# Hash attention and a gated feed-forward on one core: the softmax divisors of a pair summed in one group of four matmuls

## The chip, the cores and the metric

The kernel runs on one core of a Trainium2 chip. The metric is the device time of one execution in microseconds (us). Ten runs of the kernel before have a median of 919.51 us, from 918.42 to 920.82. One further number is used below: the execution that the profiler recorded took 918.83 us, and its span, from the first to the last instruction, is 917.0 us.

## The reference, cut to what matters

```python
# attention: 4 batches x 8 heads, S = 768, head_dim = 64, 6 hash bits
q_bits, k_bits = (q @ proj > 0), (k @ proj > 0)
mask = bucket(q_bits)[:, :, :, None] == bucket(k_bits)[:, :, None, :]
scores = np.where(mask, q @ k.T / sqrt(64), -1e9)
attn = exp(scores - max)
attn = attn / (attn.sum(-1) + 1e-9)
x = (attn @ v)                      # -> (3072, 512)
# feed-forward
h = x @ w_in                        # (3072, 2048)
g = h * erf(softplus(h))
out = g @ w_out                     # (3072, 512)
```

What the change touches is `attn.sum(-1)`: for each query the sum of its 768 exponentials, by which the row of `attn @ v` is divided.

## The kernel before, in words

The 32 heads are worked off as 16 **pairs**; the two heads of a pair (called `ab`) share the 128 partitions, 64 each. The 768 queries of a pair come in two **halves** of 384 (`HS`); `h = 0..31` counts halves over all pairs, so pair `i` has the even half `2i` and the odd half `2i+1`. The 768 keys come in six blocks of 128, and one **score stage** `n` (four of them per pair) does three of these blocks for one half.

The stages, and who does them:

- `bits_of` (L812, PE, tensor `bits`): the hash bits of a whole pair, four matmuls of 32 output rows and 384 columns, on four column quarters of the array. From there: `sign_of` (ACT, L821) writes `sg`, `weigh_bits` (DVE, L831) scales half of it, `leave_bits` (POOL, L841) sends it to DRAM (`bd`), and `place_bits` (POOL, L850) brings it back in two DMAs into one of two mask tiles `both`, which the score stages of that pair read.
- `score` (L550, PE, tensor `st`): for each key block a matmul on the mask (`both`, bf16) and one on `q` and `k` (f32), for both heads side by side. Transposed scores: keys on partitions, queries in columns.
- `exponential` (L568, ACT): `st` to `e_all`, a ring of nine blocks.
- `weigh` (L631, PE, tensor `av`): the exponentials times `v`, twelve f32 matmuls for each of the two heads in one half.
- `sum_keys` (L619, DVE): adds the six blocks of exponentials of a half to one tile of 128 partitions (`x_sum` for even halves, a part of `x` for odd ones). What is left is a sum over the partitions.
- `divisor` (L666, PE, tensor `z_ps`): that sum, by matmuls with a matrix of ones. It stands once for each half. Four matmuls, one on each column quarter: two heads times two parts of 192 queries. `keep_divisor` (L679, ACT) copies `z_ps` to `z`.
- `spread`, `gather`, `invert`, `ungather`, `widen` (SP and DVE, tensors `zd`, `zc`, `rd`, `r`), once per pair: the divisors go through DRAM to be laid over 128 partitions, are inverted, and come back broadcast. `normalise` (DVE, L752) applies them, `send` (SP, `xs`) stores the result.
- Beside this, 32 **pieces** of the feed-forward's weights are fetched by POOL (`raw`, L456) and converted by ACT (L470, L477) and DVE (L484 to L532), two pieces per pair. A piece is fetched only after the piece two before it is converted.

**What sets the order.** PE's order in the attention is written out by hand in the list `order`, and every PE operation comes after the one before it. The other engines' orders come from `arrange`, a planner that goes through the operations with a cost and a rank each and appends what can start first; on each engine instructions then run in that order. POOL's queue holds `leave_bits`, `place_bits` and the weight fetches. In the order before, half `h` reads

```python
score(2h+1), score(2h+2)      # "st"
bits((h+3)//2)                # odd h only
divisor(h-1)                  # z of the half before
weigh(2h), weigh(2h+1)        # "av"
```

so in time `st, bits, z, av` (odd half) and `st, z, av` (even half) alternate. The last half's divisor stands in the feed-forward (`late`). The feed-forward, with matmuls `M` and `X` (L1183, L1323), begins at 324.5 us of the span and is not touched.

Of the kernel before, what the change touches and what calls it, by code (L numbers as in the profile page):

```python
# [54 lines left out]
F32 = mybir.dt.float32  # L55
# [8 lines left out]
P = 128  # L64
# [129 lines left out]
def kernel(  # L194
# [11 lines left out]
    nc = tc.nc  # L206
    B, H, S, D = v.shape
    NBIT = proj2.shape[1] // 2
    NPAIR = B * H // 2
# [3 lines left out]
    HS = S // 2  # L213
# [23 lines left out]
    ones = const.tile([P, D], F32, name="ones")  # L237
# [15 lines left out]
    for ab in range(2):  # L253
        rows = slice(ab * D, ab * D + D)
        nc.vector.tensor_copy(
            out=proj_sb[rows, ab * QR : ab * QR + NBIT],
            in_=proj_in[rows, ab * NBIT : (ab + 1) * NBIT],
        )
    row = const.tile([P, 1], F32, name="row")
    nc.gpsimd.dma_start(out=row, in_=bucket)  # L260
    steps = const.tile([P, 8], F32, name="steps")
    for c, (end, factor) in enumerate(
# [12 lines left out]
            out=steps[:, c : c + 1],  # L275
# [23 lines left out]
    def bank(name):  # L299
        return misc.tile([P, 512], F32, name=name, tag="bank")  # L300
# [115 lines left out]
    def attention():  # L416
        NS = NPAIR * 4
        with (
# [19 lines left out]
            pairs = {}  # L438
            raws = {}
            NH = NPAIR * 2  # L440
# [150 lines left out]

            def last_sum(h):
                return len(sum_steps(h)) - 1 if h >= 0 else 0
# [45 lines left out]
            def home(i, what):  # L639

                if i < NPAIR - 1:
                    shape, bufs = {"x": (S, 3), "z": (HS, 1), "r": (S, 2)}[what]
                    return xst.tile([P, shape], F32, name=what, tag=what, bufs=bufs)
                rows = blocks[1][:, :, :].rearrange("p k t -> p (k t)")
                c = {"x": S, "z": 2 * S, "r": 0}[what]
                return rows[:, c : c + (HS if what == "z" else S)]
# [8 lines left out]
                    accum_out=stats[:, n, i, half : half + 1],  # L655
                )

            def divisor(h):


                i, half = divmod(h, 2)
                d = pairs[i]
                z = d["z_ps"] = bank("z_ps")[:, 0 : HS // 2]
                for n in range(4):
                    ab, part = divmod(n, 2)
                    nc.tensor.matmul(  # L666
                        out=z[n * QR : (n + 1) * QR, :],
                        lhsT=ones[:, 0:QR],
                        rhs=d["sum", half][:, 0, ab, part * HS // 2 : (part + 1) * HS // 2],
                        start=True,  # L670
                        stop=True,
                    )

            def keep_divisor(h):
                i, half = divmod(h, 2)
                d = pairs[i]
                if half == 0:
                    d["z"] = home(i, "z")
                nc.scalar.copy(  # L679
                    out=d["z"][:, half * HS // 2 : (half + 1) * HS // 2], in_=d.pop("z_ps")  # L680
                )

            def leave(h):

# [19 lines left out]
            def spread(i):  # L704

                d = pairs[i]
                zd = d["zd"] = dram.tile([2, 4, HS // 2], F32, name="zd", tag="zd")
                d["zc"] = small.tile([P, 2 * S // P], F32, name="zc", tag="zc")
                nc.sync.dma_start(
                    out=zd.rearrange("h n c -> n h c"),  # L710
                    in_=d["z"][0 : 3 * QR + 1 : QR, 0:HS].rearrange("n (h c) -> n h c", h=2),
                )

            def gather(i):
                d = pairs[i]
                nc.sync.dma_start(
                    out=d["zc"],
                    in_=d.pop("zd")
                    .rearrange("h n c -> (h n c)")
                    .rearrange("(p c) -> p c", c=2 * S // P),  # L720
                )

# [56 lines left out]
            for n in range(WARM):  # L779
                nc.tensor.matmul(  # L780
                    out=bank("warm")[:, 0 : 2 * P],
                    lhsT=warm[:, 0:P],
                    rhs=warm[:, P:HS],
                    start=True,
                    stop=True,
# [5 lines left out]
            NH = NPAIR * 2  # L791
            ops = []

            def op(fn, args, engine, cost, rank, after=(), **more):
                name = (fn.__name__,) + args
                ops.append(Op(name, engine, cost, rank, lambda: fn(*args), after=after, **more))

            def pe(fn, args, cost, after=()):
                if chain:
                    after += (chain[-1],)  # L800
                op(fn, args, "PE", cost, (0, len(chain)), after, late=0.25)
                chain.append((fn.__name__,) + args)
# [58 lines left out]
            chain = []  # L861
            order = [("score", 0)]
            for h in range(NH):
                order += [("score", n) for n in (2 * h + 1, 2 * h + 2) if n < NS]
                if h == 0:
                    order.insert(3, ("bits", 1))
                if h % 2 and (h + 3) // 2 < NPAIR:
                    order.append(("bits", (h + 3) // 2))
                if h >= 1:
                    order.append(("divisor", h - 1))  # L870
                order += [("weigh", 2 * h), ("weigh", 2 * h + 1)]
            slots = []
            for what, n in order:
                if what == "score":
                    i = n // 4
                    after = (("place_bits", i),)
                    if n == 0:
                        for c in range(2):
                            pe(plain, (n, c), 0.66)
                    for c in range(GC):  # L880
                        free = (slots[-3],) if len(slots) >= 3 else ()
                        pe(score, (n, c), 0.82 if n or c == 2 else 0.17, after + free)
                        slots.append(("exponential", n, c))
                elif what == "bits":
                    pe(bits_of, (n,), 0.92, (("start_pair", n), slots[-3]))
                    slots.append(("sign_of", n))
                elif what == "divisor":
                    pe(divisor, (n,), 0.42, (("sum_keys", n, last_sum(n)), ("keep_divisor", n - 1)))
                else:
                    h = n // 2  # L890
                    after = (("exponential", n, GC - 1),)
                    if n % 2 == 0:
                        after += (("leave", h - 1), ("leave_plain", (h - 1) // 2))
                    pe(weigh, (n,), 2.02, after)
# [18 lines left out]
            for h in range(NH):  # L913
                for k, (blocks_, _, _, where) in enumerate(sum_steps(h)):
                    after = tuple(("exponential", 2 * h + b // GC, b % GC) for b in blocks_)
                    after += (("sum_keys", h, k - 1), ("sum_keys", h - 1, last_sum(h - 1)))
                    if k == 0:
                        after += (("divisor", h - 2),)
                        if h == NH - 2:
                            after += (("measure", NPAIR - 3, 0, 1),)  # L920
                    op(sum_keys, (h, k), "DVE", 1.72 if where == 2 else 0.92, (1, 2 * h + 1, k), after)
            for h in range(NH - 1):
                i = h // 2
                op(
                    keep_divisor,
                    (h,),
                    "ACT",
                    0.34,
                    (0, 2 * h, -1),
                    (("divisor", h), ("spread", i - 1)),  # L930
                )
            for h in range(NH):
                i = h // 2
# [3 lines left out]
            for i in range(NPAIR):  # L937
                n = 4 * i
# [765 lines left out]
    with tc.manual_schedule():  # L1704
        late = attention()
        feed_forward(judge, late)
# [57 lines left out]
```

## Time and profile before

| | us |
|---|---|
| median of 10 runs | 919.51 |
| profiled execution | 918.83 |
| its span | 917.0 |
| PE busy in the span | 904.3 |
| DVE busy | 819.7 |
| ACT busy | 768.4 |
| `z_ps` matmuls (L666), passes x duration | 256 x 0.33 to 0.34, four at a time |
| `bits` matmuls (L812), passes x duration | 120 x 0.50, four at a time |
| copies `z<-z_ps` (L679) | 30 x 0.33 |

PE is TensorE's matmuls, PEld its weight loads, DVE VectorE, ACT ScalarE, POOL GpSimd, SP SyncE; a q behind a name means the engine's sequencer or queue. A row of the timeline gives the start and the length in us, the engine, the line, the operation, the tensors written and read, the shape, how many are merged, and in brackets the idle time before it and what ended it. An f32 matmul shows as two passes. Matmuls of one row can lie side by side on parts of the array, so lengths are not added up: the distance from one start to the next is what a stage costs.

### The profile page before, as it was taken

To read this page: it belongs to the slowest core of one execution; us is meant where nothing else is said; L and a number is where in the kernel's file an instruction comes from. 1 tells how busy PE (TensorE), PEld (TensorE's weight loads), DVE (VectorE), ACT (ScalarE), POOL (GpSimd) and SP (SyncE) were. 2 spreads that over 40 slices of the span, in tenths; PEclk is the share of its full clock that TensorE was granted. 3 is DMA by queue.
4 is the path that set the end of the run, shared out by engine and by line. 5 is a ranking of instruction groups with operands and counts; after the bars stand their busy time and mean duration, and the time that the engine had idled before them with its cause. 6 is when DMAs were issued, how large, how long until landed. Compare 5 with 4: busy or idle time off the path is not lost.

```text
span 917.0 us, 13120 instructions
## 1 busy us (share of the span) xinstructions
PE 904.3 (99%) x5006; PEld 658.7 (72%) x5006; DVE 819.7 (89%) x1020; ACT 768.4 (84%) x1002; POOL 46.7 (5%) x83
## 2 busy tenths in 40 slices
PE   9999999999999999999999999999999999999997
PEld 4444444444444478888888888888888888888885
DVE  4899999999898979899999799989899889988995
ACT  5788887788887839999998998899989997899892
POOL 1211111111111000000000000000000000000000
PEclk9999999999999999999999999999999999999999
DMA  8455567655673131102022112211121121011201
GB/s 205 118 154 161 158 181 196 184 144 161 178 199 107 59 122 64 46 1 104 12 70 80 36 46 69 81 35 46 70 81 35 35 75 40 36 35 46 69 35 49
DMA packets 62966, 83.05 MB, mean 91 GB/s; under 512 B 34174, under 2 KB 47342, under 8 KB 62896
## 3 DMA queue, kind: packets, MB, share of 16 engines
q1 hardware_dynamic: 56672, 64.08, 24.0%
q0 software_dynamic: 6064, 17.86, 6.1%
q8 instruction: 41, 0.67, 0.3%
q14 instruction: 29, 0.24, 0.1%
q10 hardware_dynamic: 160, 0.20, 0.1%
HBM read 64.71 MB, written 17.40 MB: 90 GB/s over the span
## 4 chain that ended last, share of the span: by engine, by line
PE 95%; DVE 2%; ACT 1%; DMA 1%; issue 0%; POOL 0%; DVEq 0%; ACTq 0%; POOLq 0%
PE M L1323 31%; PE X L1183 28%; PE st L550 16%; PE av L631 13%; PE M L1183 3%; PE z_ps L666 1%; PE bits L812 1%; ACT e_all L568 1%; PE warm L780 1%; DMA raw<-in_w_in_dram 0%; DVE e L1237 0%; DMA bd<-sg 0%; DVE h L1265 0%; DMA both<-bd 0%; PE bits L373 0%
## 5 line engine op out<-in xcount | busy, mean ns | idle before, releaser
L1250 DVE SCALAR_TENSOR_TENSOR e<-w,e 128x1024 f32<-128x1024 f32 x144 | 173.4, 1220 | 5.8 <-ACT w L1246 3.0
L568 ACT ACTIVATE e_all<-st 128x768 f32<-128x768 f32 x192 | 151.2, 813 | 14.6 <-PE st L550 14.6
L1246 ACT ACTIVATE w<-w,cq 128x1024 f32<-128x1024 f32 x144 | 160.8, 1145 | 1.9
L550 PE MATMUL st<-q,k 64*128 64x384 f32 x768 | 155.2, 483 | 0.0
L1323 PE MATMUL M<-w_out_sb,h 128*128 128x256 f32 x576 | 140.2, 379 | 0.4 <-DVE h L1265 0.4
L631 PE MATMUL av<-e_all,v 128*64 128x385 f32 (+1 forms) x768 | 131.1, 490 | 0.0
L1183 PE MATMUL X<-x,w_in_sb 128*128 128x256 f32 x512 | 121.1, 379 | 0.0
L1323 PEld LDWEIGHTS M<-w_out_sb,h 128*128 128x128 f32 x576 | 109.2, 190 | 15.9 <-DVE h L1265 1.1
L1183 PEld LDWEIGHTS X<-x,w_in_sb 128*128 128x128 f32 x512 | 97.0, 190 | 13.8 <-ACT h L1201 0.6
L631 PEld LDWEIGHTS av<-e_all,v 128*64 128x64 f32 x768 | 52.3, 136 | 67.5 <-issue 66.9
L1323 PE MATMUL M<-wt,S 128*128 128x256 f32 x384 | 93.4, 379 | 0.4 <-DVE S L1280 0.4
L550 PEld LDWEIGHTS st<-q,k 64*128 64x128 f32 x768 | 68.3, 188 | 34.6 <-issue 34.0
L1183 PE MATMUL X<-x_sum,w_sum 128*128 128x256 f32 x344 | 81.7, 380 | 1.8 <-ACT h L1201 1.8
L1323 PEld LDWEIGHTS M<-wt,S 128*128 128x128 f32 x384 | 72.9, 190 | 10.7 <-DVE S L1280 0.8
L1183 PEld LDWEIGHTS X<-x_sum,w_sum 128*128 128x128 f32 x344 | 65.0, 190 | 12.0 <-ACT h L1201 3.3
L1201 ACT COPY h<-X 128x512 f32<-128x512 f32 x85 | 49.1, 577 | 22.1 <-PE X L1183 21.2
L1227 DVE SCALAR_TENSOR_TENSOR w<-w,e 128x1024 f32<-128x1024 f32 x48 | 58.4, 1221 | 9.7 <-ACT w L1222 9.6
L550 PE MATMUL st<-both 64*128 64x384 bf16 x384 | 63.2, 324 | 1.7 <-DMA both<-bd 1.5
L1265 DVE TENSOR_TENSOR h<-h,e 128x1024 f32<-128x1024 f32 x48 | 58.0, 1220 | 5.8 <-ACT e L1261 5.5
L1241 ACT ACTIVATE w<-e 128x1024 f32<-128x1024 f32 x48 | 50.5, 1051 | 13.2 <-DVE e L1237 12.9
L1237 DVE TENSOR_TENSOR e<-e,w 128x1024 f32<-128x1024 f32 x48 | 57.5, 1219 | 2.7 <-ACT e L1233 2.6
L1205 DVE TENSOR_TENSOR h<-X,h 128x512 f32<-128x512 f32 x65 | 44.8, 690 | 16.3 <-PE X L1183 15.3
(133 smaller groups left out, 1376.6 us busy)
## 6 DMA issues: line engine op xcount, KB each, us to landing
wt<-wt SPq DMA_DIRECT2D x24, 768.0 KB, 4.1
raw<-in_w_out_dram POOLq DMA_DIRECT2D x16, 512.0 KB, 4.1
raw<-in_w_in_dram POOLq DMA_DIRECT2D x14, 512.0 KB, 4.5
v<-in_v_dram SPq DMA_DIRECT2D x32, 192.0 KB, 4.7
xs<-x SPq DMA_DIRECT2D x16, 384.0 KB, 2.6
q<-in_qkT_dram SPq DMA_DIRECT2D x30, 192.0 KB, 4.1
k<-in_qkT_dram SPq DMA_DIRECT2D x30, 192.0 KB, 4.2
r<-rd SPq DMA_DIRECT2D x30, 192.0 KB, 3.5
```

The lines of the kernel that those rows point to most:

```text
L550: nc.tensor.matmul(out=st[:, ab, 0:HS], lhsT=d["k" + src][rows, keys], rhs=d["q" + src][rows, cols], start=(part == 0), stop=(part == 1),)
L568: nc.scalar.activation(out=e[:, :, 0:HS], in_=st[:, :, 0:HS], func=AF.Exp, scale=scale)
L631: nc.tensor.matmul(out=d["av"][rows, 0:w], lhsT=d["v"][:, g * GC + c, rows], rhs=e[:, ab, 0:w], start=(g == 0 and c == 0), stop=(g == 1 an ...
L1183: nc.tensor.matmul(out=d[where][:, u, :], lhsT=a[:, kc, f : f + P], rhs=b[:, kc, :], start=(first and u == 0 and kc == 0), stop=(last and ...
L1201: nc.scalar.copy(out=quarter(p, q), in_=st[p][where])
L1227: nc.vector.scalar_tensor_tensor(out=w, in0=w, scalar=-1.0, in1=st[p]["e", v], op0=ALU.add, op1=ALU.subtract)
L1237: nc.vector.tensor_tensor(out=s, in0=s, in1=st[p].pop(("w", v)), op=ALU.subtract)
L1241: nc.scalar.activation(out=z, in_=st[p]["s", v], func=AF.Square)
L1246: nc.scalar.activation(out=q, in_=z, func=AF.Square, bias=cq[:, j : j + 1])
L1250: nc.vector.scalar_tensor_tensor(out=s, in0=st[p].pop(("q", v, j)), scalar=ERF_Q[j][1], in1=s, op0=ALU.add, op1=ALU.mult,)
L1265: nc.vector.tensor_tensor(out=h, in0=h, in1=st[p].pop(("s", v)), op=ALU.mult)
L1323: nc.tensor.matmul(out=banks[name][:, sub, :], lhsT=a[:, u, sub * P : (sub + 1) * P], rhs=b[:, u, :], start=(c == 0 and k == 0), stop=(c = ...
```

## The change

The divisor of a whole pair is made at once. Four matmuls again, on four column quarters, but now a quarter is one half and one head with all its 384 queries. It stands in the odd half's wake: at the beginning of the next even half, ahead of its scores, and the bits of the pair after the next stand right before it, so that the order is

```python
# even h, from 2 on
bits((h+2)//2); divisor(h-1)                  # both halves of pair (h-1)//2
score(2h+1), score(2h+2); weigh(2h), weigh(2h+1)
# odd h
score(2h+1), score(2h+2); weigh(2h), weigh(2h+1)
```

The last pair keeps a divisor per half, each on two quarters of 384 queries. `keep_divisor` copies 384 columns once instead of 192 twice, the DRAM tile `zd` becomes four rows of 384, and the planner gets the new costs and dependences: the sums of an even half begin only after the divisor of the pair before.

```diff
-            def divisor(h):
-                i, half = divmod(h, 2)
-                d = pairs[i]
-                z = d["z_ps"] = bank("z_ps")[:, 0 : HS // 2]
-                for n in range(4):
-                    ab, part = divmod(n, 2)
-                    nc.tensor.matmul(
-                        out=z[n * QR : (n + 1) * QR, :],
-                        lhsT=ones[:, 0:QR],
-                        rhs=d["sum", half][:, 0, ab, part * HS // 2 : (part + 1) * HS // 2],
+            def divisor(h, halves=None):
+                d = pairs[h // 2]
+                halves = halves or ((h % 2,) if h >= NH - 2 else (0, 1))
+                z = d["z_ps"] = bank("z_ps")[:, 0:HS]
+                for half in halves:
+                    for ab in range(2):
+                        row = (2 * half + ab) * QR
+                        nc.tensor.matmul(
+                            out=z[row : row + QR, :],
+                            lhsT=ones[:, 0:QR],
+                            rhs=d["sum", half][:, 0, ab, :],
...
-                nc.scalar.copy(
-                    out=d["z"][:, half * HS // 2 : (half + 1) * HS // 2], in_=d.pop("z_ps")
-                )
+                rows = slice(half * D, half * D + D) if h >= NH - 2 else slice(0, P)
+                nc.scalar.copy(out=d["z"][rows, :], in_=d.pop("z_ps")[rows, :])
...
             for h in range(NH):
+                if h and h % 2 == 0:
+                    if (h + 2) // 2 < NPAIR:
+                        order.append(("bits", (h + 2) // 2))
+                    order.append(("divisor", h - 1))
                 order += [("score", n) for n in (2 * h + 1, 2 * h + 2) if n < NS]
                 if h == 0:
                     order.insert(3, ("bits", 1))
-                if h % 2 and (h + 3) // 2 < NPAIR:
-                    order.append(("bits", (h + 3) // 2))
-                if h >= 1:
+                if h == NH - 1:
                     order.append(("divisor", h - 1))
                 order += [("weigh", 2 * h), ("weigh", 2 * h + 1)]
...
-                    pe(divisor, (n,), 0.42, (("sum_keys", n, last_sum(n)), ("keep_divisor", n - 1)))
+                    pe(
+                        divisor,
+                        (n,),
+                        0.7,
+                        (("sum_keys", n, last_sum(n)), ("keep_divisor", n - (2 if n % 2 else 1))),
+                    )
...
                     if k == 0:
-                        after += (("divisor", h - 2),)
+                        after += (("divisor", h - (1 if h % 2 == 0 else 2)),)
...
-            for h in range(NH - 1):
+            for h in (*range(1, NH - 2, 2), NH - 2):
                 i = h // 2
                 op(
                     keep_divisor,
                     (h,),
                     "ACT",
-                    0.34,
-                    (0, 2 * h, -1),
+                    0.48,
+                    (0, 2 * h + 1, -1),
```

More of the change, by code (lines that the diff above doesn't have):

```diff
@@ L656, in measure @@
                 )
-            def divisor(h):
-                i, half = divmod(h, 2)
-                d = pairs[i]
-                z = d["z_ps"] = bank("z_ps")[:, 0 : HS // 2]
-                for n in range(4):
-                    ab, part = divmod(n, 2)
-                    nc.tensor.matmul(
-                        out=z[n * QR : (n + 1) * QR, :],
-                        lhsT=ones[:, 0:QR],
-                        rhs=d["sum", half][:, 0, ab, part * HS // 2 : (part + 1) * HS // 2],
-                        start=True,
-                        stop=True,
-                    )
+            def divisor(h, halves=None):
[9 more added lines that the diff above has]
+                            rhs=d["sum", half][:, 0, ab, :],
+                            start=True,
+                            stop=True,
+                        )
             def keep_divisor(h):
@@ L676, in keep_divisor @@
                 d = pairs[i]
-                if half == 0:
+                if "z" not in d:
                     d["z"] = home(i, "z")
-                nc.scalar.copy(
-                    out=d["z"][:, half * HS // 2 : (half + 1) * HS // 2], in_=d.pop("z_ps")
-                )
+                rows = slice(half * D, half * D + D) if h >= NH - 2 else slice(0, P)
+                nc.scalar.copy(out=d["z"][rows, :], in_=d.pop("z_ps")[rows, :])
             def leave(h):
@@ L706, in spread @@
                 d = pairs[i]
-                zd = d["zd"] = dram.tile([2, 4, HS // 2], F32, name="zd", tag="zd")
+                zd = d["zd"] = dram.tile([4, HS], F32, name="zd", tag="zd")
                 d["zc"] = small.tile([P, 2 * S // P], F32, name="zc", tag="zc")
[L709 to L712, printed above, removed]
+                nc.sync.dma_start(out=zd, in_=d["z"][0 : 3 * QR + 1 : QR, :])
             def gather(i):
@@ L718, in gather @@
                     in_=d.pop("zd")
-                    .rearrange("h n c -> (h n c)")
+                    .rearrange("h c -> (h c)")
                     .rearrange("(p c) -> p c", c=2 * S // P),
@@ L887, in attention @@
                 elif what == "divisor":
-                    pe(divisor, (n,), 0.42, (("sum_keys", n, last_sum(n)), ("keep_divisor", n - 1)))
+                    pe(
[3 more added lines that the diff above has]
+                        (("sum_keys", n, last_sum(n)), ("keep_divisor", n - (2 if n % 2 else 1))),
+                    )
                 else:
```

## The prediction

> **What bounds the kernel.** I read the page's busy times and chain first, then the list of PE's waits, then PE's timeline over one pair, and last the timelines of DVE and POOL beside it.
>
> ```profile
> PE 904.3 (99%) x5006; PEld 658.7 (72%) x5006; DVE 819.7 (89%) x1020; ACT 768.4 (84%) x1002; POOL 46.7 (5%) x83
> PE 95%; DVE 2%; ACT 1%; DMA 1%; issue 0%; POOL 0%; DVEq 0%; ACTq 0%; POOLq 0%
> ```
>
> PE is the bound: what shortens its row of stages shortens the kernel, as long as nothing that it waits for comes later. PE's own waits are 1.5 us on `both<-bd` (pair 1), 0.6 us before the feed-forward, and little more. From 66 us to the end of the attention it does not wait once, and repeats this (cost of a stage = distance to the next start):
>
> ```profile
> 106.83 0.81 PE L550 MATMUL st<-q,k 64*128 64x384 f32 x4
> 107.57 0.52 PE L812 MATMUL bits<-q,proj_q 128*32 128x384 f32 x2
> ...
> 107.92 0.49 PE L812 MATMUL bits<-q,proj_q 128*32 128x384 f32 x2
> ...
> 108.24 0.51 PE L666 MATMUL z_ps<-x_sum,ones 128*32 128x192 f32 x8
> 108.68 4.09 PE L631 MATMUL av<-e_all,v 128*64 128x384 f32 x24
> 112.71 0.34 PE L550 MATMUL st<-both 64*128 64x384 bf16 x2
> ...
> 116.75 0.33 PE L550 MATMUL st<-both 64*128 64x384 bf16 x2
> 116.92 0.81 PE L550 MATMUL st<-q,k 64*128 64x384 f32 x4
> 117.66 0.53 PE L666 MATMUL z_ps<-x,ones 128*32 128x192 f32 x8
> 118.12 4.10 PE L631 MATMUL av<-e_all,v 128*64 128x385 f32 x24
> 122.15 0.34 PE L550 MATMUL st<-both 64*128 64x384 bf16 x2
> ```
>
> bits 0.67, z 0.44, av 4.03, st 4.95, z 0.46, av 4.03, and the st before it 4.95: 19.53 us a pair. Each stage ends in a switch of the array's shape (the forms 64\*128, 128\*32, 128\*64), and that is not free. A score block takes 0.81, but the last, 116.75 to 117.66, takes 0.91: 0.10 for st to z. The two rounds of `bits` are 0.35 and 0.32 long, so a 384-column round is 0.32 and the first after a switch 0.02 to 0.03 more. z has two rounds of half that, 0.32, and costs 0.44: 0.12 for z to av. av has twelve rounds of 0.32 (3.86) and costs 4.03: 0.17 for its slow first round and the switch to st.
>
> **The change, part by part.** (1) *Four quarters of 384 instead of twice four of 192.* The columns streamed are the same: twice 0.32 before, once 0.65 after. (2) *The order.* Before there are six switches in a pair (st-bits, z-av, av-st, st-z, z-av, av-st), after it five (av-bits, z-st, st-av, av-st, st-av); bits to z is no switch either way. With each stage's cost as now: bits 0.67, z 0.32 + 0.32 + 0.12 = 0.76, then st 4.95, av 4.03, st 4.95, av 4.03: 19.39 us. That is 0.14 less a pair, for the 15 pairs with a joint divisor **-2.10 us**. av-bits, z-st and st-av stand nowhere in the trace of before; by the neighbouring switches one switch is worth 0.09 (bare) to 0.17 (with the slow first round of av), so the term lies between -1.4 and -2.6. I take the sum of the rows. (3) *The last pair* fills only two quarters with 384 columns: 0.65 instead of 0.32, twice, once before the last av and once inside the feed-forward, both on PE's path: **+0.64 us**.
>
> [...] The rows: the rounds of 192 columns are half as long as those of 384 (z 0.32 for two, `bits` 0.32 for one), so fewer and longer matmuls gain nothing in themselves. [...]
>
> (4) *POOL's queue.* The built order has two weight fetches ahead of the third pair's bits, where before the second of them stood behind `place_bits`. That one cost something:
>
> ```profile
> 58.80 1.14 POOL L456 DMA_DIRECT2D raw<-in_w_in_dram  x2
> 63.35 0.43 DVE L484 TENSOR_SCALAR top<-raw 128x512 int32<-128x512 int32 x1 [0.74 <-DMA raw<-in_w_in_dram]
> 63.41 0.69 ACT L470 ACTIVATE keep<-raw 128x512 f32<-128x512 f32 x1 [3.51 <-DMA raw<-in_w_in_dram]
> ```
>
> ACT stood still 3.51 us behind it, its exponentials came late, and PE's score stage at 63.25 took 5.26 instead of 4.95. Fetched at about 54 us, the piece is there in time: **-0.31 us** on PE (bounds 0 and -0.31), and DVE gets 0.74 us ahead, 1.1 with the 0.39 us that it waits for ACT just after.
>
> (5) *New wait one: z needs the odd half's sums earlier.* The divisor stood 5.0 us behind the odd av; now it follows that av at 0.67 (the bits). In front of everything: the next scores, exponentials and copies queue behind this matmul. DVE is packed (19.2 to 19.4 us busy in every 20 us from 80 to 160 us), so its sums end where its fixed order lets them end. In the built order the work ahead of each odd sum is the same as before to within 0.1 us, except for three pairs where it is 0.4 to 1.4 us less. So sums keep their times, while PE comes earlier by 1.11 us (the bits and z that left the first odd half) and 0.14 for each pair. The tightest pair:
>
> ```profile
> 89.15 4.09 PE L631 MATMUL av<-e_all,v 128*64 128x384 f32 x24
> 92.16 0.32 DVE L831 TENSOR_SCALAR sg<-sg,weight_q 64x384 bf16<-64x384 bf16 x1
> 92.51 0.96 DVE L619 TENSOR_TENSOR x<-x 128x768 f32<-128x768 f32 x1
> ```
>
> The sum ends at 93.47, or 93.1 without the `sg` row, which the built order puts behind it. PE's av would end at 93.18 - 1.84 (1.11 + 0.31 + 0.14 x 3) = 91.3 and z want the sum at 92.0: 1.1 us of waiting, less DVE's 0.7 to 1.1 of lead. The next tightest (190.6) adds 0.3 or nothing, since a wait of PE moves all that comes later. Bounds 0 and 1.4.
>
> (6) *New wait two: the bits leave PE 4 us later* against the scores that need them. DVE's `weigh_bits` runs 3.5 to 4.5 us later in the built order; then
>
> ```profile
> 113.59 0.32 DVE L831 TENSOR_SCALAR sg<-sg,weight_q 64x384 bf16<-64x384 bf16 x1
> 114.20 0.55 POOL L841 DMA_DIRECT2D bd<-sg  x1 [7.30 <-DVE sg L831]
> 118.62 1.15 POOL L850 DMA_DIRECT2D both<-bd  x2 [3.87 <-PE z_ps L666]
> both<-bd POOLq DMA_DIRECT2D x30, 21.0 KB, 3.6
> ```
>
> 0.3 + 4.4 + 0.6 + 3.6 = 8.9 us from the end of `weigh_bits` to the landed mask. The first score on it begins 0.67 + 0.76 + 4.95 + 4.03 + 2.5 = 12.9 us after its bits began. `weigh_bits` would end (its row's place between two sums, with DVE's times of before) 3.9 to 5.5 us after the bits began, so 7.5 to 9.2 us are left, 7.5 to 7.9 in five pairs. With DVE's lead that becomes 8.6 to 9.0. It is a close thing: 0 to 1.4 us by the median trip; with the shortest DMAs (1.9 and 2.1 of 3.6) nothing. The loads of `q`, `k`, `v`, which begin where the odd av ends, lie beside the first DMA as now but have mostly landed by the second, so I lean to the short side. (5) and (6) do not add up: who waits for one has more room for the other. I take **+0.3 us** for both together; the bounds are 0 and 3.5 (1.4 and 2.1, the longest trip of 9.6 in 7.5 us, without any lead).
>
> [...]
>
> (7) *At nothing:* ACT's one copy of 384 for two of 192 (0.33 each), 80% busy there; the round of `zd`, `zc`, `rd`, `r`, whose spread now starts some 4 us earlier while its DVE rows stand about 3 us earlier; later `place_bits` push every second weight fetch back by 3 to 4 us, and its piece still lay 3.4 to 8 us unused. If that cover goes, ACT and DVE wait a few tenths.
>
> Sum: -2.10 + 0.64 - 0.31 + 0.3 = **-1.47 us**. Against the profiled execution 918.83 - 1.47 = 917.4; that run lies 0.7 below the median of 919.51, so the median to expect is **918.0 us**. Measurement can tell about 0.2% here, 1.84 us; the forecast is within it.
>
> **Rivals.** *A, the full gain:* no new wait, a switch worth up to 0.17: -1.8 to -2.3 us, 917.5 at the median. For it: DVE's lead; against: the two tight places. *B, slower, by the mask's trip:* at the second half of the odd score stage PE waits for `both<-bd`. Every us that the trip exceeds its room costs PE one us, once. If DVE gets no lead and the trip is as long as the longest now, the waits are 3.5 us and the sum is -1.46 + 3.5 = +2.0: 921.5. It decides from 1.8 us of waits on (no gain), from 3.6 on it is slower by 0.2%. Against it: such a trip must coincide with the tightest pairs. *C, not four at a time:* the last two quarters wait for DVE and the first two do not, and they could run one after the other, 0.65 more a pair, +9.7 - 1.5: 927.7. Against it: the `bits` have a wait before their third matmul too and take 0.67.
>
> **Chances.** Forecast, -0.5 to -1.84: 0.47; A 0.34; waits that eat the gain without turning it, 0.08; B 0.08; C 0.03. So faster by over 0.2% 0.34, within 0.55, slower 0.11. Range 916.8 to 920.6: A's gain with a low median at one end, most of the waits' bounds at the other.
>
> **What would show it.** In the profile after: 128 passes on L666 of about 0.49; distances bits-z 0.67, z-st 0.76, st-av 4.95, and 19.39 a pair; no `raw` wait near 63 us. Wrong would be: PE waits for `x<-x` at z (5), for `both<-bd` in the odd scores (6), or a st-av distance over 5.05.

## The result, and the profile after

The changed kernel takes 924.33 us (median of 14 runs, 922.23 to 927.04), the kernel before 919.55 us beside it on the same chips (50 runs). The ratio is 1.0051, with a 95% interval of 1.0041 to 1.0061: slower by half a per cent, outside the predicted range. The profiled execution took 925.31 us with a span of 923.5, 6.5 us more than the one of before. In the texts on record below, T1, T2 and so on are the theories of the time; each is told in words here.

The page of the changed kernel, its busy row and the shares of its chain of waits (followed back from the last instruction to whatever released each step); those of before stand in the prediction:

```profile
PE 905.7 (98%) x4878; PEld 658.0 (71%) x4878; DVE 819.7 (89%) x1020; ACT 768.8 (83%) x987; POOL 47.3 (5%) x83
PE 90%; DVE 5%; DMA 3%; SPq 1%; ACT 1%; issue 0%; POOL 0%; DVEq 0%; ACTq 0%; POOLq 0%
```

PE's busy time has hardly moved (904.3 before), but its share of the chain has fallen from 95% to 90%, and DMA has 3% where it had 1%: PE now waits for something. The part that the change meant is as it was worked out. PE's timeline over one pair of the changed kernel:

```profile
108.19 4.09 PE L631 MATMUL av<-e_all,v 128*64 128x384 f32 x24
112.21 0.52 PE L808 MATMUL bits<-q,proj_q 128*32 128x384 f32 x2
...
112.88 0.49 PE L666 MATMUL z_ps<-x_sum,ones 128*32 128x384 f32 x2
112.90 0.49 PE L666 MATMUL z_ps<-x,ones 128*32 128x384 f32 x2
...
113.64 0.34 PE L550 MATMUL st<-both 64*128 64x384 bf16 x2
...
118.59 4.10 PE L631 MATMUL av<-e_all,v 128*64 128x385 f32 x24
```

av to bits is 4.02, bits to z 0.67, z to st 0.76, st to av 4.95. An undisturbed pair takes 19.39 us instead of 19.53. The two z of one round (112.88 and 112.90) start beside each other on different column quarters. What is new stands in the list of PE's waits:

```profile
PE st L550 <- DMA both<-bd: 4.0, 1, 4.0
```

One wait of 4.0 us for a mask: it is pair 9's, in the second half of an odd score stage, the place that rival B named. PE's timeline there (in brackets the idle time ahead of the row and what ended it):

```profile
182.94 0.81 PE L550 MATMUL st<-q,k 64*128 64x384 f32 x4
187.77 0.67 PE L550 MATMUL st<-both 64*128 64x384 bf16 x2 [4.01 <-DMA both<-bd]
188.06 1.65 PE L550 MATMUL st<-q,k 64*128 64x384 f32 x4
```

The rows after the wait are twice as long as their like (0.67 for 0.33, 1.65 for 0.81). Sums by 4 us stretches tell why; the columns are the stretch, its length, busy time of PE, PEld, DVE, ACT and POOL, the granted clock (the share of its full speed at which TensorE was clocked), the busy share of the DMA engines and GB/s:

```profile
184.00:188.00 4.00, 0.23 (x2) 0.17 (x4) 3.83 (x10) 0.61 (x1) 0.04 (x1) 0.89 0.99 359
188.00:192.00 4.00, 4.00 (x20) 2.52 (x21) 3.86 (x4) 2.25 (x5) 0.56 (x1) 0.68 0.66 184
```

The clock is 0.89 and 0.68 in two stretches of 4 us, 1.72 us of clock missing, which is 3.4 us at half clock; in stretches of 1 us from 187 on it is 0.57, 0.50, 0.50 and 0.72, and 1.00 in the ones on either side. The stage of 181.16 takes 10.58 us instead of 4.95: 4.01 of standing still and 1.62 of slow clock. The DMA share of 0.99 points at the cause of the wait. SP's queue and POOL's queue in the changed kernel at that time:

```profile
181.91 0.43 SPq L330 DMA_DIRECT2D x<-xs  x1
```

```profile
182.32 1.15 POOL L846 DMA_DIRECT2D both<-bd  x2 [4.17 <-PE st L550]
```

and in the kernel before:

```profile
176.03 1.57 SPq L330 DMA_DIRECT2D x<-xs  x1
```

```profile
176.18 1.15 POOL L850 DMA_DIRECT2D both<-bd  x2 [4.53 <-DMA bd<-sg]
```

`x<-xs` is `load_x`, 1 MB of the feed-forward's first input. In the changed kernel it goes out 0.4 us ahead of the mask's way back, and the chain of waits has 5.4 us for that 21 KB transfer, where the median of its kind in this run is 2.1:

```profile
182.32 5.40 DMA both<-bd
```

Before, the two go out together too (176.03 and 176.18), but there the two transfers of the mask landed in 2.6 and 3.0 us, and they were sent some 6.5 us ahead of their use. So a mask issued behind the load is not always late: before, the load's row lasts 1.57 us and the mask's begins 0.15 us into it; in the changed kernel the load's lasts 0.43 us and is all but over when the mask's begins. No run shows why the one mask took 3 us and the other 5.4.

A table of the time from the end of the score stage that starts at 22 us (so that the first loads don't count) to the feed-forward's first product. Stretches are distances from one stage's start to the next:

| | from | to | us | PE's stages that are longer than regular, extra us |
|---|---|---|---|---|
| before | 29.14 | 324.46 | 295.32 | st 63 +0.31 |
| changed | 29.61 | 329.81 | 300.20 | z 92 +1.03; st 123 +0.27; z 171 +0.10; st 181 +5.63; z(30) +0.31 |

Before, less 15 x 0.14, less the 0.31 at 63 us, plus the last column's 7.34 gives 300.25: nothing is left over (z(30) is the z of half 30, the last pair's first). Behind this the last pair's second half adds 0.31, and the rest of the 6.5 us lies in the start (0.47) and behind the last products (0.8).

### The profile page after: what moved, and what is told of

The parts are those of the page before. It is cut to its first block, busy times and chain, and to the rows that moved or that the text cites. A ratio compares the mean times of both kernels' runs of the same rounds, so it can differ in the third digit from the quotient of the medians.

```text
span 923.5 us, 12846 instructions
## 1 busy us (share of the span) xinstructions
PE 905.7 (98%) x4878; PEld 658.0 (71%) x4878; DVE 819.7 (89%) x1020; ACT 768.8 (83%) x987; POOL 47.3 (5%) x83
## 4 chain that ended last, share of the span: by engine, by line
PE 90%; DVE 5%; DMA 3%; SPq 1%; ACT 1%; issue 0%; POOL 0%; DVEq 0%; ACTq 0%; POOLq 0%
PE M L1326 31%; PE X L1186 27%; PE st L550 14%; PE av L631 12%; PE M L1186 3%; PE z_ps L666 1%; PE bits L808 1%; DVE x L619 1%; DMA both<-bd 1%; SPq L358 1%; DMA q<-in_qkT_dram 1%; DMA zd<-z 1%; DVE x_sum L619 0%; DMA bd<-sg 0%; DVE e L1240 0%
```

## The experiments

The medians here stand beside runs of the kernel before on the same chip; a ratio is to those.

**1. The changed kernel, with x's load late.** The load moves behind the widening of pair 13, about 305 us; nothing else.

```diff
-            op(load_x, (0,), "SP", 1.1, (1, 0), (("send", JP - 1), ("start_pair", 10)), late=4.0)
+            op(load_x, (0,), "SP", 1.1, (1, 0), (("send", JP - 1), ("widen", NPAIR - 3)), late=4.0)
```

> The changed kernel with one difference: the load of the feed-forward's first input block (1 MB, x<-xs) stands behind the widening of pair 13, near 305 us, instead of just ahead of the way back of pair 9's mask. Theory T1 (one collision: mask 9 queues behind that load, PE stands 4.0 us, and its clock is halved for 3.4 us after): the stall of 5.6 us in the score stage at 181 us is gone, all st-av distances 4.95 but small ones, median 918.6 to 919.6. Rival T2 (the moved bits are simply too late, some other mask will be late instead): another wait on both<-bd of over 1 us appears and the time stays above 922.

920.70 us, ratio 1.0015 (1.0002 to 1.0029). The waits of PE in this run:

```profile
PE st L550 <- DMA both<-bd: 0.2, 1, 0.2
```

The 4.0 us are gone, the clock's fall with them (1.00 from 180 to 200 us, 0.91 in the changed kernel), and the changed kernel is 3.3 us faster by the two ratios. But it doesn't become faster than before: from the score stage on it takes 295.45 us, as long as before (295.32). Its stages show where the 2.1 us went: z 92 +0.87, st 122 +0.42, st 180 +0.40, z 190 +0.49, st 239 +0.11. The three in st are masks again (pairs 6, 9 and 12), the two in z are sums.

**2. The bits at their old place.** The change with `bits` ahead of the odd half's av again; the divisor stays joint.

```diff
-                    if (h + 2) // 2 < NPAIR:
-                        order.append(("bits", (h + 2) // 2))
                     order.append(("divisor", h - 1))
...
+                if h % 2 and (h + 3) // 2 < NPAIR:
+                    order.append(("bits", (h + 3) // 2))
```

> The changed kernel with the bits back at their old place, behind the odd half's scores; the joint divisor stands alone behind the odd av, and the 1 MB load keeps its place in its queue. T1 and T2 both: no wait on both<-bd after pair 1, so no stall of several us; six switches a pair again, 19.53 us a pair, and the divisor comes 0.67 us earlier against DVE's sums, so waits of 1.5 to 2.5 us in all at z: 920.5 to 922. Rival T3 (the joint divisor's waits for DVE are the main cost, not the mask): 923 or more.

924.54 us, ratio 1.0061 (1.0045 to 1.0076), slower than T1 and T2 expected and in the range of the rival T3. No score stage waits for a mask after pair 1, so the late bits are what brought the masks near the edge. But z waits more: from z to the next scores it is 4.17 us at 93.17, and 1.05 to 1.52 at three others, where it is 0.79 without a wait. In this order z's waits are the cost, 5.0 us in all; in the changed kernel they are 1.1. The longest of VectorE's waits up to 325 us, in total, times and longest:

```profile
DVE zc L722 <- DMA zc<-zd: 6.7, 5, 4.0
```

VectorE stands 6.7 us at the head of its queue for `zc<-zd`, the divisors on their way back (6 KB). The longest of these waits, 4.00 us, ends at 88.86, ahead of the sum that the z at 93.17 needs; SP's queue has the first leg of that round right behind the loads of q, k and v.

**3. Late load, and the last pair on four quarters.** Experiment 1, with the last two divisors in four matmuls of 192 columns as before.

```diff
+                if h >= NH - 2:
+                    for n in range(4):
+                        ab, part = divmod(n, 2)
+                        nc.tensor.matmul(
+                            out=z[n * QR : (n + 1) * QR, 0 : HS // 2],
+                            lhsT=ones[:, 0:QR],
+                            rhs=d["sum", h % 2][:, 0, ab, part * HS // 2 : (part + 1) * HS // 2],
+                            start=True,
+                            stop=True,
+                        )
+                    return
...
```

> e1 with the last pair's two divisors on four quarters of 192 queries again, as in the kernel before. By the terms of the prediction it gains 0.32 us twice: 0.64 below e1, so 918.0 to 919.0 under T1; in the profile z-av and z-M distances of 0.46 instead of 0.77.

920.79 us, ratio 1.0012 (0.9995 to 1.0029): no difference to experiment 1 that the medians can tell, though the profile shows z(30) at 0.47 again instead of 0.77. Four stages are long: z 92 +0.77, st 122 +0.35, st 180 +0.48, z 190 +0.68. Their sum, 2.28, is the 2.1 + 0.31 that the change frees, to 0.13 us. What they wait for stands at the weight loads ahead of the matmuls, in the order of the four:

```profile
92.88 0.14 PEld L677 LDWEIGHTS z_ps<-x,ones 128*32 128x32 f32 x4 [0.64 <-DVE x L619]
124.79 0.09 PEld L550 LDWEIGHTS <-both 64*128 64x128 bf16 x1 [0.40 <-DMA both<-bd]
183.43 0.09 PEld L550 LDWEIGHTS <-both 64*128 64x128 bf16 x1 [0.52 <-DMA both<-bd]
191.31 0.14 PEld L677 LDWEIGHTS z_ps<-x,ones 128*32 128x32 f32 x4 [0.55 <-DVE x L619]
```

**4. The kernel before, with x's load late.** The same edit of the load as in experiment 1.

> The kernel before with only the 1 MB load moved to the same late place as in e1. T1: masks there have some 4 us of room, the load does not stand in their way, so the time is that of the kernel before, 919.5, within 0.2%. If the load costs something wherever it stands early (T4), it is faster by 1 us or more, and e1's gain would not be the collision alone.

919.54 us, ratio 0.9997 (0.9984 to 1.0010). In the kernel before, the load's place is worth nothing: experiment 1 won its 3.3 us from the meeting of load and mask, not from the load.

**5. The load ahead of another mask.** The changed kernel, with the load put just ahead of pair 8's way back. If the meeting is the cause, the wait must move with the load.

```diff
-            op(load_x, (0,), "SP", 1.1, (1, 0), (("send", JP - 1), ("start_pair", 10)), late=4.0)
+            op(load_x, (0,), "SP", 1.1, (1, 0), (("send", JP - 1), ("place_bits", 8)), late=4.0)
```

> e1 with the 1 MB load put on purpose just ahead of another mask's way back (pair 8, near 160 us). T1: both<-bd of pair 8 lands some 5.4 us after its issue instead of 2.1 to 2.8, PE waits about 2 us at the second half of the odd score stage near 163.5 us, and the time is 2 to 4 us above e1's 920.7 (more if the clock is halved after the wait). If the stall in the changed kernel had another cause than the load (T2, or the late return of r), nothing happens there and the time is e1's.

921.56 us, ratio 1.0025 (1.0012 to 1.0038). SP issued the load at 161.42, POOL the mask at 161.94. The chain of waits and PE's timeline:

```profile
161.94 5.41 DMA both<-bd
```

```profile
167.40 0.54 PE L550 MATMUL st<-both 64*128 64x384 bf16 x2 [2.09 <-DMA both<-bd]
```

Again 5.4 us for the mask, now that of pair 8, and PE waits there and no more at pair 9. It stands 2.09 us and not 4.01, since this mask was earlier by its own, and the stage takes 7.41 us, 2.46 more than regular. The cause is confirmed, the price less so: by the medians the kernel is 0.9 us slower than in experiment 1, where 2 to 4 were expected. Three later waits of experiment 1 (0.40, 0.49 and 0.11) are gone for it. The profiled execution, 1.5 us above the median, also has z at 92 longer by 2.53, behind 2.69 us in which VectorE waits for `zc<-zd` at 66; that is 95 us ahead of the load and no part of the meeting.

**6. The planner's costs as measured.** Experiment 3, with the planner's VectorE costs set to the durations of the trace (sums 0.99 and 1.79 for 0.92 and 1.72, weight pieces 1.19 to 1.46 for 1.05 to 1.30, and so on); no instruction is added or taken.

```diff
-                op(add_rest, (n,), "DVE", 1.3, (2, n, 2), (("mask_bits", n),))
+                op(add_rest, (n,), "DVE", 1.46, (2, n, 2), (("mask_bits", n),))
...
```

> e3 with the planner's DVE costs raised to what the trace shows (sums 1.79 and 0.99 instead of 1.72 and 0.92, weight conversion 1.19, 1.19, 1.46 instead of 1.05, 1.1, 1.3, and so on); only DVE's and others' order changes, no work. e3's profile still has 2.3 us of small waits: z at 92 and 190 us 1.5 and 1.4 instead of 0.76, score stages at 122 and 180 us 5.3 and 5.4 instead of 4.95. Theory T5 (the order of DVE's queue puts weight work ahead of sums that PE now wants earlier): these waits go, 2 us below e3. Rival T6 (DVE has no spare time at all, whatever the order): the waits turn up later in the attention or before the feed-forward, within 0.5 us of e3.

925.42 us, ratio 1.0063 (1.0049 to 1.0077). The attention now runs without a long stage: 292.86 us, the full gain. But the sums that the feed-forward needs have been pushed behind it. PE's timeline:

```profile
322.33 3.72 PE L1207 MATMUL M<-x,w_in_sb 128*128 128x256 f32 x16 [0.58 <-ACT x L703]
331.74 5.67 PE L1207 MATMUL M<-x_sum,w_sum 128*128 128x256 f32 x16 [5.68 <-DVE x_sum L342]
```

PE stands still for 5.68 us, and the next row takes 5.67 us for the 3.72 of its like, since the clock has fallen meanwhile (0.61 and 0.53 in the two stretches of 4 us from 328 on). VectorE's work was moved, not made less, and the time came back at the next place that waits for it. But the new order also lost some of VectorE's time. Its sums from 20 to 320 us (columns as above) and its largest wait there:

```profile
20.00:320.00 300.00, 299.31 (x2096) 139.30 (x2094) 273.46 (x371) 241.00 (x433) 44.60 (x76) 1.00 0.58 155
DVE ev L709 <- ACT x L703: 8.0, 12, 1.2
```

VectorE is busy for 273.46 us there, where experiment 3 has 279.33 (shown with experiment 10), and stands 8.0 us for ScalarE's copies, where experiment 3 has 0.4. It was 5.9 us behind in its work, about what PE then waits for.

**7. Part of VectorE's work on GpSimd.** Experiment 3, with the eight `presum_weights` on GpSimd.

```diff
-                nc.vector.tensor_tensor(out=out_, in0=one_, in1=two_, op=op_)
+                nc.gpsimd.tensor_tensor(out=out_, in0=one_, in1=two_, op=op_)
```

> e3 with the eight sums of weights (presum_weights, 1.22 us each on DVE, 9.8 us in all) moved to GpSimd, which is busy 5%. T5 and T6 both: DVE's sums end earlier from 88 us on, PE's waits at z vanish, 2 us below e3. Rival T7 (POOL's queue then holds masks and weight fetches behind these sums, or GpSimd slows DVE's own instructions): new waits on both<-bd or longer DVE instructions, at or above e3.

933.24 us, ratio 1.0142 (1.0127 to 1.0158). The eight take 2.4 to 3.8 us each there, instead of 1.2, and VectorE's own sums become longer. One group of VectorE's sums here, and then in experiment 3:

```profile
L619 DVE TENSOR_TENSOR x<-x,e_all 128x768 f32<-128x768 f32 (+1 forms) x24 | 36.7, 1545 | 1.4
```

```profile
L619 DVE TENSOR_TENSOR x<-x,e_all 128x768 f32<-128x768 f32 (+1 forms) x24 | 30.5, 1288 | 1.4
```

With the other two groups of sums into `x` (31.1 for 27.1, 18.4 for 14.4) VectorE lost 14.2 us to be rid of 10. The groups of sums into `x_sum` kept their times (26.7, 26.4 and 14.3 us for 26.7, 26.3 and 14.3); what made the ones into `x` longer was not shown. The move was no relief, and told nothing on whether relief would help.

**8 and 9. A plan with the sums ranked ahead of the late weights,** for the changed kernel (experiment 6 and this) and for the kernel before.

```diff
-                    op(leave_plain, (i,), "DVE", 0.19, (0, 2 * h, 0), (("weigh", 2 * h + 1),))
+                    op(leave_plain, (i,), "DVE", 0.19, (0, 2 * h, 0), (("weigh", 2 * h + 1), ("leave", h)))
...
-                    (2, 31, k),
+                    (2, 8 * (k // 4) + 7, 3 + k),
...
-                op(presum_x, (0, k), "DVE", 0.72, (2, 31, 8 + k), ...
+                op(presum_x, (0, k), "DVE", 0.72, (2, 7, 11 + k), ...
```

> The kernel of the run with the planner's costs of VectorE as measured, with two more entries put right in the plan: leave_plain is planned only after ScalarE's copy of the same half (on the chip it waits for that copy anyway, about 7.7 us at the head of VectorE's queue in all), and the sums for the feed-forward (presum_weights, presum_x) are ranked ahead of the late pieces of the second weight. T8 (the new stage's loss was a matter of the plan, and the sums ahead of the feed-forward were only misplaced): attention without waits as in that run, first feed-forward product at 322 to 323 us and no wait of 5.7 us for x_sum behind it; 916.5 to 918.5 us, faster than before. T9 (VectorE's whole work up to the feed-forward is the bound, whatever its order): the 5 us turn up again, at x_sum or at the first results of the feed-forward that wait for VectorE; 920 to 925 us.

> The kernel before with the same entries of the plan (VectorE's costs as measured, leave_plain after ScalarE's copy, the sums for the feed-forward ahead of the late pieces), and with no other part of the change. T8 in the form that the change is worth its 2.1 us in a fitting plan: waits in the attention go as far as before has them (under 1.5 us in all), 918 to 919.5 us, and about 2 us more than the changed kernel in the same plan. T10 (the plan is worth as much without the change): within 0.7 us of the changed kernel in the same plan. T9: as with the other, 920 us or more.

927.60 us, ratio 1.0094 (1.0079 to 1.0108), and 929.00, ratio 1.0111 (1.0092 to 1.0129): both worse. In the changed kernel the attention takes 293.42 us, and then late weight pieces fill VectorE's queue and ScalarE's, with the feed-forward's copies behind them:

```profile
332.52 6.26 PE L1207 MATMUL M<-x_sum,w_sum 128*128 128x256 f32 x16 [6.43 <-ACT h L1225]
```

The time turns up a third time. VectorE is busy for 272.43 us from 20 to 320 us here, 6.9 less than in experiment 3. So neither of the two plans keeps the gain, but each also leaves VectorE idle for longer, by about what PE then waits for: they don't show that no order could keep it, nor that VectorE's whole work is the bound in any order. The pair does not tell what the change is worth in one plan either: the two medians are 1.4 us apart, between the two expectations, and the kernel before kept x's load early where the changed one has it late. Its profiled execution (935.82 us, the slowest of six) waits 3.74 us for a mask near 28 us and 4.31 us for ScalarE ahead of the second products of the feed-forward.

**10 and 11. VectorE with less to do.** Experiment 3 and the kernel before, each in its own unchanged order, but without `rest`, 0.69 us for each of 32 weight pieces. The low part of the weights is left out in both. The sum that took `rest` in becomes a maximum of `top` with itself, so that no other instruction is added or taken.

```diff
-                nc.vector.scalar_tensor_tensor(
-                    out=rest,
-                    in0=low.bitcast(U32),
-                    scalar=2.0**-52,
-                    in1=unit[:, :].bitcast(F32),
-                    op0=ALU.mult,
-                    op1=ALU.mult,
-                )
...
```

> The changed kernel with x's load late and the last pair on four quarters, in the very same order of instructions, but one VectorE instruction fewer for each of the 32 weight pieces (rest, 0.69 us each, 22 us before the feed-forward's start): the low part of the weights is left out. T11 (VectorE, 93% busy up to 320 us in the kernel before, is the second bound there, and the 2.1 us that TensorE gains are given back in waits for it): the waits at z and at the score stages go, first feed-forward product at 322 to 322.6 us instead of 324.4, total 2 us below that run, 916 to 918 us, and 1.5 us or more below the kernel before with the same instruction left out. T12 (the waits come from the order, from ScalarE or from transfers): first product stays at 324 or later, total within 0.7 us of that kernel.

> The kernel before in its own order with the same VectorE instruction left out of each weight piece (so the low part of the weights is left out). T11: it has little to win, since TensorE's own work sets its length: its first feed-forward product stays at 324 to 324.5 us, total 918 to 919.5 us, at most 0.7 us below before. T12: the same, and the changed kernel with that instruction left out gives the same time as this one. If VectorE bound the kernel before as well, this one falls by 2 us or more too, and neither theory is right about where the bound lay.

916.83 us, ratio 0.9971 (0.9957 to 0.9984), and 919.55, ratio 0.9996 (0.9985 to 1.0007). This tells the theories apart. The same relief is worth nothing in the kernel before and 3.8 us (by the ratios) in the changed one, which with it is 2.7 us faster than the kernel before with it. In time from the score stage on: 292.86 and 295.01. Experiment 3 takes 295.13 there, so the relief is worth 2.27 us in the profiles, as much as the four waits of experiment 3; no stage accounts for what the 3.8 has beyond that (the twelve runs of experiment 3 spread from 918.76 to 925.26). From before's 295.32 the prediction's rows give 295.32 - 2.10 - 0.31 = 292.91 for the one; without the change but with the 0.31 they give 295.01 for the other. The busy sums from 20 to 320 us (columns as above), of experiment 3 and of 10:

```profile
20.00:320.00 300.00, 298.70 (x2078) 137.69 (x2076) 279.33 (x378) 243.56 (x433) 44.63 (x76) 1.00 0.59 154
```

```profile
20.00:320.00 300.00, 298.33 (x2088) 137.38 (x2086) 260.74 (x350) 243.74 (x432) 46.27 (x76) 1.00 0.57 155
```

The third busy column is VectorE's: 279.33 and 260.74 of 300 us; the kernel before has 279.70 and experiment 11 258.12. At 93% it runs just beside PE, at 87% it runs ahead. How this reaches both kinds of wait is seen at pair 9: `weigh_bits`, which sends the mask off, in experiment 3 and in experiment 10:

```profile
175.56 0.32 DVE L848 TENSOR_SCALAR sg<-sg,weight_q 64x384 bf16<-64x384 bf16 x1
```

```profile
170.94 0.32 DVE L842 TENSOR_SCALAR sg<-sg,weight_q 64x384 bf16<-64x384 bf16 x1
```

It ends 5.8 us after the bits began in the first, and 2.0 us after in the second, with the same instructions ahead of it except for `rest`. What is shown is that VectorE's work, in the order that it has, makes the waits. A lighter piece also lets the sum behind it start earlier, so the two runs do not tell whether the amount of work or its place in the queue is what counts.

**12. A relief that leaves nothing out.** Experiment 3, with `leave_plain` (one column scaled) on ScalarE, ahead of ScalarE's copy of the same half.

```diff
-                nc.vector.tensor_scalar(
-                    out=d["ev"],
-                    in0=d["av"][:, HS : HS + 1],
-                    scalar1=EPS,
-                    scalar2=None,
-                    op0=ALU.mult,
+                nc.scalar.activation(
+                    out=d["ev"], in_=d["av"][:, HS : HS + 1], func=AF.Copy, scale=EPS
                 )
```

> The changed kernel with x's load late and the last pair on four quarters, with leave_plain (0.15 to 0.19 us, at the head of VectorE's queue it also waits for ScalarE's copy of the same half) on ScalarE ahead of that copy, in the plan too. T11: VectorE gets some 3 us of work and up to 8 us of waits back over the attention, so part of the 2.1 us is kept: first product at 322.5 to 323.8 us, 917.5 to 919.5 us, faster than before by 0.1 to 0.2%. T12 (order and ScalarE matter more): ScalarE's copies come 0.2 us later each, which delays the release of av, no gain or a loss: 920 us or more.

920.64 us, ratio 1.0018 (1.0003 to 1.0034); the gain did not come. VectorE's busy time from 20 to 320 us fell by 2.5 us only, to 276.83, and the plan was laid out anew, with VectorE waiting 4.8 us for `zc<-zd` where experiment 3 has 1.3. This run decides nothing, since the relief is small and the order another. No kernel that computes all of the reference was found that is faster than before.

## Why the prediction was wrong

Step by step:

- **(1) and (2), right.** 19.39 us a pair, each distance as written, though three of the switches had no row of their own before. The quarters run side by side: rival C did not come.
- **(3), right.** z(30) and z(31) take 0.77 for 0.46, twice 0.31; the prediction had 0.64 for both.
- **(4), right on PE, wrong on VectorE's lead.** The stall at 63 us is gone. The 0.7 to 1.1 us of lead that VectorE was to keep are not there: at 65.36 it waits 1.15 us for `zc<-zd`, a round that (7) had at nothing, and pair 3's sum ends at 93.43, with 93.47 before.
- **(5), mis-sized.** The place and the mechanism were right: z waits for the sum at pair 3, first of all. The prediction had 1.1 less the lead; without the lead 1.03 were measured.

The lines of the changed kernel for that place, VectorE's wait first, then its sum, then PE's z:

```profile
65.36 0.17 DVE L722 TENSOR_SCALAR zc<-zc 128x12 f32<-128x12 f32 x1 [1.15 <-DMA zc<-zd]
```

```profile
92.47 0.96 DVE L619 TENSOR_TENSOR x<-x 128x768 f32<-128x768 f32 x1
```

```profile
93.49 0.84 PE L666 MATMUL z_ps<-x,ones 128*32 128x384 f32 x4 [0.21 <-DVE x L619]
```

- **(6) with (7), the step that failed.** The sum had +0.3 us for the waits of (5) and (6) together; the four of them measured 7.03 (1.03, 0.27, 0.10 and 5.63), and 5.63 of that is the stage of one mask. For that wait the prediction gave 0 to 2.1 us, from a trip of 8.9 us against a room of 7.5 to 9.2 (its own figures, 12.9 less 3.9 to 5.5, give 7.4 to 9.0). Measured at pair 9, the trip from the end of `weigh_bits` to PE's restart was 10.5 us (177.29 to 187.77) and the room 6.5 (to 183.75). VectorE's rows on the way, with what they waited for:

```profile
154.22 1.02 DVE L748 SCALAR_TENSOR_TENSOR x<-x,ev,r 128x768 f32<-128x768 f32 x1 [1.70 <-DMA r<-rd]
175.92 1.02 DVE L748 SCALAR_TENSOR_TENSOR x<-x,ev,r 128x768 f32<-128x768 f32 x1 [0.80 <-DMA r<-rd]
176.97 0.32 DVE L827 TENSOR_SCALAR sg<-sg,weight_q 64x384 bf16<-64x384 bf16 x1
```

  Two things were missing. First, the room: `weigh_bits` of pair 9 ended 6.7 us after its bits began (at 170.64) and not 3.9 to 5.5, since VectorE lost 1.7 and 0.8 us to `r<-rd` on the way. With a way back of 2.1 us the second half of the mask, issued at 182.89, would have been there at 185.0 and PE, free at 183.75, would have waited some 1.3 us, inside the bounds (in experiments 1 and 3, without the load, that stage was long by 0.40 and 0.48). Second, the load. (7) costed the DMA rounds at nothing and never named `x<-xs`: the diff doesn't touch it, but it stands in SP's queue, its place there follows from the plan, and it met the mask. That made 1.3 into 4.0, and the half clock made 4.0 into 5.6. Rival B had the place and the mechanism, but took the trip's price from the longest trip seen before (9.6 us for all of it), and had no term for the load or for the clock.
- **What it left out altogether: VectorE as the second bound.** The prediction read VectorE's 19.2 to 19.4 us in every 20 and used it for two tight places. It did not ask what happens when PE needs the same 280 us of VectorE's work 2.1 us sooner. Without the load's collision (experiments 1 and 3) the change is worth nothing: the 2.1 us return in waits for sums and masks (four of them in experiment 3), and VectorE sets the time of both. So the forecast of -1.47 us would have failed by 2 to 3 us even without the load. Experiments 10 and 11 show this for the order as it is; in the two other orders that were tried, 6 and 8, the time turned up at another place.

What stays open: whether some order, with lighter VectorE work that still computes all of the weights, keeps the 2 us. Experiments 6, 7, 8 and 12 tried for it, and none did.

## What to carry to other kernels

Before a stage is shortened on the engine that bounds, look at the next engine's busy time in that stage: here, at 93%, it gave back what the first one gained, and only a kernel with that work taken away showed what the change itself was worth. When a plan decides the order, every DMA of every queue near a moved step counts, also those that the diff does not touch: here a 1 MB load 0.4 us ahead of a small transfer that PE needed cost more than the whole change gains. A wait of PE can be dearer than its length: 4.01 us of it cost 5.63.

## What the runs showed of the hardware

- A 21 KB transfer issued by POOL 0.4 to 0.5 us behind a 1 MB load issued by SP took 5.4 us to land, twice (pair 9, pair 8), where the median of its kind in the changed kernel's run is 2.1. In the kernel before, issued 0.15 us behind the same load, it took 2.6 and 3.0.
- With a wait of 4.01 us, which ended at 187.77, the clock was 0.57, 0.50, 0.50 and 0.72 in the four stretches of 1 us from 187 on, 3.4 us at half clock in all. In experiment 6, with a wait of 5.68 us, which ended at 331.74, it was 0.61 and 0.53 in the two stretches of 4 us from 328 on, about 6.9 us if all of it was at half clock, part of it while PE still stood. After a wait of 2.09 us (experiment 5) it stayed at 1.00.
- Four column quarters of one shape, of which two stand behind another engine's result, ran side by side at pair 4, where PE did not wait for it: 0.49 us a pass, two starts 0.01 to 0.02 us apart (112.88 and 112.90, 113.21 and 113.22). At pair 3, where the sum came late, the two began 1.03 us behind the others (92.46 and 93.49).
- A sum of 128 x 1024 f32 took 2.4 to 3.8 us on GpSimd and 1.2 on VectorE, and the means of VectorE's sums into `x` rose by 15 to 28% in that run.
